# Tail keys' weighted values as 64-row matmuls, and the other weighted-value matmuls fed between feed-forward matmuls

## The chip, the cores and the metric

One core of a Trainium2 chip runs the whole program. Its engines work side by side, each through its own queue in order: PE (matmuls, with weight loads shown apart as PEld), DVE (elementwise), ACT (activation functions, and here copies out of PSUM and the output DMAs), POOL (here it only issues loads) and SP (here it issues transposing DMAs). Matmuls write to PSUM, eight banks of 512 float32 numbers in each of 128 partitions. The metric is the device time of one execution in microseconds (us), the median of three runs.

## The reference

Attention with a bias that depends on the distance of query and key, and behind it a feed-forward layer that multiplies two projections:

```python
scores = q @ k.T / 8 + bias[|i - j|]     # 8 batches, 8 heads, 576 positions, head width 64
attn   = exp(scores) / sum(exp(scores))  # over the keys
x      = attn @ v                        # heads side by side: 4608 tokens of 512
out    = ((x @ w_a) * (x @ w_b)) @ w_out # 512 -> 1536 -> 512
```

The softmax subtracts the row's maximum first, which changes nothing in exact arithmetic; the kernel leaves it out.

## The kernel before

**Tiling of the attention.** The kernel works in pairs of heads: 8 batches of 4 pairs, 32 pairs. A pair's two heads lie on partitions 0 to 63 and 64 to 127 of the transposed queries and keys. The 576 positions are four tiles of 128 and a tail of 64. Scores are computed with keys on the partitions, so that the exponentials are already what the product with v needs as its stationary operand.

For a pair `p` the parts are:

- `qk(p, 0)` and `qk(p, 2)` (L408): scores of key tiles 0, 1 and of 2, 3 against the 512 main queries. Each key tile takes two 64-row matmuls, one for each head, into the two banks of one PSUM tile of the pool `ps_sc` (two such tiles). `ex` (L436) is the exponential on ACT, 1024 columns, into an `at` tile; `mul` (L442) multiplies it on DVE by the bias factor exp(bias).
- the rows: in `qk(p, 2)` also the 64 tail queries against the four main key tiles, eight 64-row matmuls of 64 columns (L424) into two banks, one of each head. `ex_rows` (L428) reads the two banks, `mul_rows` (L533) applies the bias.
- `qk_tail` (L484): the tail keys of both heads (64 partitions each, stacked to 128) against all queries; `ex_tail` (L508) is their exponential, 640 columns, into `att`; `mul_tail` (L526, instruction L531) multiplies its last 256 columns, those of query tile 3 and of the tail queries, by the bias factor. The earlier columns need none.
- the weighted values `av(p, jqs)` (L559): `av_mm` and then `av_norm`. For a query tile `jq`, first the tail keys (L568): 128 rows, the two heads' tail keys one above the other, against a block-diagonal `vt` of 2 x 65 columns. Each 65th column is ones, so that it gives the softmax's denominator. Then for each head and key tile a matmul of 65 columns (L578). For `jq` 4, the tail queries of both heads, four matmuls of 130 columns (L572). Everything accumulates in one PSUM bank with a place for each tile and head, from the pool `ps_av`, which has one bank. `av_norm` (L583) divides on DVE into `XG`: a reciprocal (L589), a product (L591), and for the tail queries two small products (L596). `av(p, (0, 1, 2))` and `av(p, (3, 4))` are two such blocks.
- `t_x` (L600): two transposing DMAs from SP bring `XG` into `xn`, the feed-forward's input.

**Feed-forward.** 4608 tokens are nine chunks of 512. A chunk is 36 units in a fixed list: 24 projections, a first (`ff_a`: four matmuls of 512 columns into a PSUM bank, L642, and a copy on ACT to `ha`, L649) and a second (`ff_b`: four matmuls, and on DVE the product `g` of bank and `ha`, L652) in turn; and 12 output units, four matmuls each (L679), three to a bank, with a copy and an output DMA on ACT after each third. All these banks come from the pool `ps_ff`, which has two.

**Order.** The kernel writes the order of every queue out by hand; nothing is scheduled. Pairs 0 to 7 and the first chunk's projections are an opening of their own. From L868 a loop runs over steps `s` = 8 to 32. Step `s` computes the scores of pair `s` and, for `s` above 8, the weighted values of pair `s - 1`, and places nine feed-forward units between them. `U` is one unit. For `s` not divisible by four the order is:

```python
qk(s,0) ex(s,0) | U1 ex(s,1) av(s-1,(0,1,2)) U2 mul(s,0) U3 mul(s,1)
qk(s,2) + rows, ex(s,2) ex_rows | U4 ex(s,3) U5 mul(s,2) mul_rows
av(s-1,(3,4)) t_x(s-1) U6 U7 mul(s,3) | qk_tail ex_tail U8 U9 mul_tail
```

For `s` divisible by four the second block of weighted values and two more units come before `qk(s,2)`. Loads of later batches and transposing DMAs of queries and keys are issued at a step's end.

With nine units to a step and 36 to a chunk, steps repeat in fours. I call them by `s` modulo four:

| kind | steps | units U1 to U9 |
|---|---|---|
| 1 | 9, 13, ... 29 | first, second, first, ... first |
| 2 | 10, 14, ... 30 | second, first, ... second |
| 3 | 11, 15, ... 31 | first, second, ... second (six), then three output units |
| 0 | 12, 16, ... 28 | nine output units |

Step 32 has no scores: it computes the last pair's weighted values among output units, and transposes on PE (`tr_x`, into `trb`, the one bank of the pool `ps_tr`). The same `trb` takes the first head's rows in each step, a bank of `ps_av` the second's.

Of the kernel before, what the change touches and what calls it, by code (L numbers as in the profile page):

```python
# [13 lines left out]
def kernel(  # L14
# [11 lines left out]
    nc = tc.nc  # L26
    FP32 = mybir.dt.float32
    BF16 = mybir.dt.bfloat16
# [279 lines left out]

    st = [dict() for _ in range(NP)]

    trb = ps_tr.tile([128, 1024], BF16, tag="tr", name="trb")
    turn = [0]

    def tr_half():
        turn[0] ^= 1
        return trb[:, 512 * turn[0]:512 * turn[0] + 512]

    def copy(eng, out, in_):
        if eng is nc.scalar:
# [88 lines left out]
    def qk(p, t0, ts=None):  # L408
        qT, kT, _ = operands(p)
        st[p].setdefault("at", [None] * NM)  # L410
        for t in ts or (t0, t0 + 1):
            ps = ps_sc.tile([128, 2, 512], FP32, tag="sc", name=f"qk{p}_{t}")
            for hh in range(2):
                r = slice(64 * hh, 64 * hh + 64)
                nc.tensor.matmul(out=ps[:, hh, :], lhsT=kT[r, t, :], rhs=qT[r, :, :],  # L415
                                 start=True, stop=True)
            st[p]["ps", t] = ps
        if shared(p) and t0 == 2:
            z = operands(p)[2]
            rows = (trb.bitcast(FP32), ps_av.tile([128, 512], FP32, tag="av", name=f"qr{p}"))  # L420
            for t in range(NM):
                for hh in range(2):
                    r = slice(64 * hh, 64 * hh + 64)
                    nc.tensor.matmul(out=rows[hh][:, ST * t:ST * t + ST], lhsT=kT[r, t, :],  # L424
                                     rhs=z[r, 0, ST * hh:ST * hh + ST], start=True, stop=True)
            st[p]["rows"] = rows

    def ex_rows(p):  # L428
        st[p]["att"] = at = att[p % 2]
        for hh in (1, 0):  # L430
            nc.scalar.activation(
                out=at[:, 0:512].rearrange("p (t h c) -> p h t c", h=2, t=NM)[:, hh, :, :],
                in_=st[p]["rows"][hh][:, 0:256].rearrange("p (t c) -> p t c", t=NM),
                func=ACTF.Exp, scale=scale)

    def ex(p, t):  # L436
        ps = st[p]["ps", t]
        at = atp.tile([128, 2, SM], BF16, tag="at", name=f"at{p}_{t}")
        nc.scalar.activation(out=at[:, :, :], in_=ps[:, :, :], func=ACTF.Exp, scale=scale)  # L439
        st[p]["at"][t] = at  # L440

    def mul(p, t):  # L442
        at, w = st[p]["at"][t], W_sb[p % 4]
        nc.vector.tensor_tensor(out=at[:, :, :], in0=at[:, :, :],  # L444
                                in1=w[:, :, S - 1 + t:S - 1 + t - SM:-1], op=MULT)
# [95 lines left out]
    def weights(p, t, hh, jq):  # L541
        if p >= 4:
            return st[p]["at"][t][:, hh, 128 * jq:128 * jq + 128]
        o = 256 * (t % 2) + 128 * (jq % 2)
        return st[p]["at", jq // 2, t // 2][:, hh, o:o + 128]

    def weights_last(p, t):
        return st[p]["att"][:, 2 * ST * t:2 * ST * t + 2 * ST]

    def weights_tail(p, jq):  # L550
        if jq == 4:
            o = 512 + main_tail(p)
            return st[p]["att"][:, o:o + 2 * ST]
        if p < 4 and jq < 2:
            return atk[:, p, 128 * jq:128 * jq + 128]
        o = 512 + 128 * (jq if p >= 4 else jq - 2)
        return st[p]["att"][:, o:o + 128]
# [2 lines left out]
        av_mm(p, jqs)  # L560
        av_norm(p, jqs)

    def av_mm(p, jqs, pool=None, tag="av"):
        b, hp = divmod(p, 4)
        i = b % 2
        pav = (pool or ps_av).tile([128, 3, 2, Dh + 1], FP32, tag=tag, name=f"av{p}_{jqs[0]}")
        for slot, jq in enumerate(jqs):
            nc.tensor.matmul(out=pav[:, slot, :, :], lhsT=weights_tail(p, jq),  # L568
                             rhs=vt[i][:, :, hp, :], start=True, stop=True)
            if jq == 4:  # L570
                for t in range(NM):
                    nc.tensor.matmul(out=pav[:, slot, :, :], lhsT=weights_last(p, t),  # L572
                                     rhs=vm[i][:, 2 * hp:2 * hp + 2, t, :], start=False,
                                     stop=True, skip_group_check=True)
                continue
            for hh in range(2):
                for t in range(NM):
                    nc.tensor.matmul(out=pav[:, slot, hh, :], lhsT=weights(p, t, hh, jq),  # L578
                                     rhs=vm[i][:, 2 * hp + hh, t, :], start=False,
                                     stop=True, skip_group_check=True)  # L580
        st[p]["pav", jqs[0]] = pav

    def av_norm(p, jqs):  # L583
        pav = st[p]["pav", jqs[0]]
# [15 lines left out]
    def t_x(p, jqs=range(5), eng=None):  # L600
        b, hp = divmod(p, 4)
        c0 = SM * B + ST * b
        if 4 <= p < NP - 1:
            nc.sync.dma_start_transpose(
                out=xn_sb[hp][:, SM * b:SM * b + SM].rearrange("d (j c) -> d j c", j=4),
                in_=XG[p % 2][:, 0:4, :, :].rearrange("p j h d -> p (j h d)"))
            nc.sync.dma_start_transpose(
                out=xn_sb[hp][:, c0:c0 + ST],
                in_=XG[p % 2][0:ST, 4, :, :].rearrange("p h d -> p (h d)"))
            return  # L610
        tr_x(p, jqs)
        copy_x(p, jqs, eng)
# [16 lines left out]


    ff = {"late": False, "n": 0}

    def ff_bank(name):
        ff["n"] += 1
# [4 lines left out]
    def ff_in(w, kind, c, df, lo, n):  # L639
        ps = ff_bank(f"{kind}{c}_{df}_{lo}")  # L640
        for mc in range(NMC):
            nc.tensor.matmul(out=ps[:, 0:n], lhsT=w[df // 4][:, mc, 128 * (df % 4):128 * (df % 4) + 128],  # L642
                             rhs=xn_sb[mc][:, 512 * c + lo:512 * c + lo + n],
                             start=(mc == 0), stop=(mc == NMC - 1))
        ff[kind, df, lo] = ps

    def ff_ha(c, df, lo, n):
# [26 lines left out]
    def ff_o_mm(c, tt, part):  # L674
        if part == 0:
            ff["po", tt] = ff_bank(f"po{c}_{tt}")
        po = ff["po", tt]
        for df in range(4 * part, 4 * part + 4):
            nc.tensor.matmul(out=po[:, :], lhsT=g_sb[df][:, 128 * tt:128 * tt + 128],  # L679
                             rhs=wo_sb[:, df, :], start=(df == 0), stop=(df == NDF - 1))  # L680

    def ff_o_out(c, tt):
        ob = ob_last if (c, tt) == (0, 2) else wrk.tile([128, DM], FP32, tag="ob", name=f"ob{c}_{tt}")
# [43 lines left out]
    def v_next(s):  # L727
        if s % 4 == 0:
            v_in(s // 4, 0, 4)
        if s % 4 == 2:  # L730
            v_in(s // 4, 4, 8)
# [136 lines left out]
    for s in range(8, NP + 1):  # L868
        new = s < NP
        U = "unit"  # L870
        A = lambda *jq: (lambda: av(s - 1, jq) if s > 8 else None)
        steps = []
        if new:
            steps += [lambda: (qk(s, 0), ex(s, 0))]
        if new:
            head = [U, lambda: ex(s, 1), A(0, 1, 2), U, lambda: mul(s, 0), U,
                    lambda: mul(s, 1)]
            late = [A(3, 4), lambda: t_x(s - 1), U]
            if s == 8:
                late = [U]  # L880
            pair = [lambda: v_next(s), lambda: (qk(s, 2), ex(s, 2), ex_rows(s)), U,
                    lambda: ex(s, 3), U, lambda: mul(s, 2), lambda: mul_rows(s)]
            tail = [lambda: (qk_tail(s), ex_tail(s)), U, U, lambda: mul_tail(s)]
            if s % 4 == 0:
                steps += head + late + [U] + pair + [lambda: mul(s, 3)] + tail
            else:
                steps += head + pair + late + [U, lambda: mul(s, 3)] + tail
        else:
            ff["late"] = True
            steps += [A(0, 1, 2), U, U, U, A(3, 4), lambda: t_x(s - 1, (0, 1, 2)), U, U, U,  # L890
                      lambda: t_x(s - 1, (3, 4)), U, U, U]
        b = s // 4 + 1
        if s % 4 == 2 and b < B:
            t_half(b, 0)
        if s % 4 == 0 and 2 <= b - 1 < B:
            t_half(b - 1, 1)
        if s % 4 == 1 and 2 <= b < B:
            load_vt(b)
        for bb in range(3, B):
            for g in range(2):  # L900
                if s == load_slot[bb] + (2 - (bb < 5)) * g:
                    load_half(bb, g)
        quota = 9
        seen, put = 0, 0
        nu = sum(1 for x in steps if x is U)
        for x in steps:
            if x is U:
                seen += 1
                n = (quota * seen + nu - 1) // nu - put
                put_units(n)  # L910
                put += n
            else:
                x()
# [31 lines left out]
```

## Time and profile before

| | |
|---|---|
| time, median of 3 runs | 413.51 us (412.92 to 413.57) |
| profiled execution, first to last instruction (its span) | 412.1 us |
| granted clock of the matrix engine, mean over the span | 1.000 |
| PE busy | 401.5 us, 3420 matmuls |
| DVE busy | 240.6 us |
| ACT busy | 252.0 us |
| feed-forward projections, 880 matmuls (L642) | 23% + 23% of the chain that ended last |
| output matmuls (L679) | 22% of that chain |
| weighted values (L578, L568, L572) | 8% + 2% + 2% of that chain |
| one step of the loop, from start to start | 11.0 us |

Only a part of the profile's time is that of the program's own instructions: the time of a run also holds what lies before the first and after the last. Of the profiled execution no time beside its span is recorded; the median of the runs is 1.4 us above it. A matmul's recorded duration holds its way through the array, and matmuls overlap; what one costs is the distance from its start to the next one's start. A line such as `L578 ... x8` stands for eight instructions that follow each other. In a timeline the brackets give how long an engine was idle before the instruction and what ended that.

### The profile page before, as it was taken

Reading aid. Unit: us, or ns where it says so; the run is one execution under the profiler, and the core shown is the slowest. Engines: PE = TensorE matmul, PEld = TensorE weight load, DVE = VectorE, ACT = ScalarE, POOL = GpSimd, SP = SyncE. Lnnn points to the kernel's source line nnn. Section 1 sums busy time; section 2 is a strip of 40 time slices with the busy share of each in tenths; the row PEclk is TensorE's granted clock in tenths of the full one; section 3 lists DMA queues with packets and bytes.
Section 4 is the critical chain, followed back from the end, with each engine's and each line's share of the span. In section 5 each row is a group of like instructions: output and inputs, shape, how many; then the busy total and the mean of one; then the engine's idle time right before and its main releaser. Section 6 shows DMA issues by size and latency. Waiting matters only on the chain.

```text
span 412.1 us, 8718 instructions
## 1 busy us (share of the span) xinstructions
PE 401.5 (97%) x3420; PEld 209.6 (51%) x3471; DVE 240.6 (58%) x568; ACT 252.0 (61%) x386; POOL 131.4 (32%) x188
## 2 busy tenths in 40 slices
PE   7999999999999999999999999999999999999996
PEld 3476656455554555455445555555445454444443
DVE  4799997366755765476646764567547652421320
ACT  5898992577748665667557765767476642322321
POOL 5966466887029400960069004300000000000000
PEclk9999999999999999999999999999999999999999
DMA  9999999999969924994199908960520012002004
GB/s 152 185 204 197 206 137 148 166 184 131 91 127 157 141 40 91 151 127 94 35 159 150 120 17 136 117 92 17 117 67 17 16 40 78 0 5 98 2 2 102
DMA packets 135962, 42.36 MB, mean 103 GB/s; under 512 B 113544, under 2 KB 131176, under 8 KB 135920
## 3 DMA queue, kind: packets, MB, share of 16 engines
q0 software_dynamic: 81120, 19.88, 54.9%
q1 hardware_dynamic: 49456, 12.61, 19.9%
q10 hardware_dynamic: 5344, 9.31, 7.1%
q8 instruction: 27, 0.44, 0.5%
q14 instruction: 15, 0.12, 0.1%
HBM read 39.23 MB, written 9.45 MB: 118 GB/s over the span
## 4 chain that ended last, share of the span: by engine, by line
PE 95%; DMA 1%; ACT 1%; issue 1%; DVE 0%; ACTq 0%; SPq 0%
PE pb L642 23%; PE pa L642 23%; PE po L679 22%; PE av L578 8%; PE qk L415 7%; PE av L568 2%; PE av L572 2%; PE qkh L455 1%; PE qkt L488 1%; DMA xn<-in_k_dram 1%; PE trb L330 1%; PE trb L424 1%; PE trk L330 1%; ACT ath L461 0%; PE qkt L494 0%
## 5 line engine op out<-in xcount | busy, mean ns | idle before, releaser
L439 ACT ACTIVATE at<-qk 128x1024 bf16<-128x1024 f32 x112 | 113.4, 1029 | 27.4 <-DMA out_dram<-ob 10.3
L652 DVE TENSOR_TENSOR g<-pb,ha 128x512 bf16<-128x512 f32 (+1 forms) x114 | 75.6, 663 | 74.8 <-PE pb L642 58.5
L642 PE MATMUL pb<-xn,wb 128*128 128x512 bf16 (+1 forms) x440 | 111.1, 368 | 0.8
L642 PE MATMUL pa<-xn,wa 128*128 128x512 bf16 (+1 forms) x440 | 110.8, 368 | 0.7
L649 ACT ACTIVATE ha<-pa 128x512 f32<-128x512 f32 (+1 forms) x114 | 66.3, 581 | 67.6 <-PE pa L642 63.8
L679 PE MATMUL po<-wo,g 128*128 128x512 bf16 x403 | 95.5, 379 | 0.8
L444 DVE TENSOR_TENSOR at<-at,W 128x1024 bf16<-128x1024 bf16 x112 | 75.0, 685 | 22.4 <-ACT at L439 22.3
L642 PEld LDWEIGHTS <-wa 128*128 128x128 bf16 x456 | 41.2, 98 | 46.6 <-issue 6.8
L642 PEld LDWEIGHTS <-wb 128*128 128x128 bf16 x456 | 40.6, 98 | 42.9 <-issue 4.7
L679 PEld LDWEIGHTS <-g 128*128 128x128 bf16 x420 | 38.8, 98 | 44.9 <-issue 2.5
L684 ACT ACTIVATE ob<-po 128x512 f32<-128x512 f32 x34 | 20.4, 600 | 40.2 <-PE po L679 30.1
L578 PE MATMUL av<-vm,at 128*128 128x65 bf16 x896 | 41.2, 193 | 0.0
L578 PEld LDWEIGHTS <-at 128*128 128x128 bf16 x896 | 37.4, 97 | 6.1
L174 POOL DMA_DIRECT2D vt<-in_v_dram x12 | 7.4, 622 | 101.9 <-PE av L572 101.1
L136 POOL DMA_DIRECT2D qn<-in_q_dram x48 | 36.6, 825 | 9.2 <-PE trb L501 6.9
L589 DVE RECIPROCAL rc<-av 128x6 f32<-128x6 f32 (+1 forms) x64 | 11.9, 186 | 45.7 <-PE av L578 41.1
L145 POOL DMA_DIRECT2D kn<-in_k_dram x48 | 36.2, 800 | 2.6 <-DMA qn<-in_q_dram 1.6
L568 PE MATMUL av<-vt,att 128*128 128x130 bf16 x152 | 33.6, 221 | 0.2
L415 PE MATMUL qk<-QB,KB 64*128 64x512 bf16 x192 | 29.1, 381 | 0.3
L591 DVE TENSOR_TENSOR XG<-av,rc 128x384 bf16<-128x384 f32 (+2 forms) x64 | 27.2, 425 | 2.2
L515 ACT ACTIVATE att<-qkt 128x640 bf16<-128x640 f32 x24 | 16.8, 701 | 13.0 <-PE qkt L489 13.0
L568 PEld LDWEIGHTS <-att 128*128 128x128 bf16 x152 | 14.9, 98 | 6.4
(105 smaller groups left out, 322.8 us busy)
## 6 DMA issues: line engine op xcount, KB each, us to landing
out_dram<-ob ACTq DMA_DIRECT2D x31, 256.0 KB, 2.9
vn<-in_v_dram POOLq DMA_DIRECT2D x16, 256.0 KB, 5.7
kn<-in_k_dram POOLq DMA_DIRECT2D x48, 64.0 KB, 4.9
qn<-in_q_dram POOLq DMA_DIRECT2D x48, 64.0 KB, 4.1
wa<-in_moe_w_a_dram POOLq DMA_DIRECT2D x3, 512.0 KB, 8.9
wb<-in_moe_w_b_dram POOLq DMA_DIRECT2D x3, 512.0 KB, 8.3
wo<-in_moe_w_out_dram POOLq DMA_DIRECT2D x1, 1536.0 KB, 15.7
xn<-XG SPq DMA_TRANSPOSE x52, 3.5
```

Of the source, the lines that this page charges most:

```text
L136: nc.gpsimd.dma_start(out=by_tile(qn[b % 2])[:, h0 // 4, t, :, :], in_=q[b, h0:h1, 128 * t:128 * t + 128, :].transpose([1, 0, 2]))
L145: nc.gpsimd.dma_start(out=by_tile(kn[b % 2])[:, h0 // 4, t, :, :], in_=k[b, h0:h1, t:SM:NM, :].transpose([1, 0, 2]))
L415: nc.tensor.matmul(out=ps[:, hh, :], lhsT=kT[r, t, :], rhs=qT[r, :, :], start=True, stop=True)
L439: nc.scalar.activation(out=at[:, :, :], in_=ps[:, :, :], func=ACTF.Exp, scale=scale)
L444: nc.vector.tensor_tensor(out=at[:, :, :], in0=at[:, :, :], in1=w[:, :, S - 1 + t:S - 1 + t - SM:-1], op=MULT)
L568: nc.tensor.matmul(out=pav[:, slot, :, :], lhsT=weights_tail(p, jq), rhs=vt[i][:, :, hp, :], start=True, stop=True)
L578: nc.tensor.matmul(out=pav[:, slot, hh, :], lhsT=weights(p, t, hh, jq), rhs=vm[i][:, 2 * hp + hh, t, :], start=False, stop=True, skip_grou ...
L591: nc.vector.tensor_tensor(out=xg[:, jqs[0]:jqs[0] + m, :, :], in0=pav[:, 0:m, :, 0:Dh], in1=rc[:, 0:m, :].unsqueeze(3).to_broadcast([128, ...
L642: nc.tensor.matmul(out=ps[:, 0:n], lhsT=w[df // 4][:, mc, 128 * (df % 4):128 * (df % 4) + 128], rhs=xn_sb[mc][:, 512 * c + lo:512 * c + lo ...
L649: nc.scalar.activation(out=ha[:, 0:n], in_=ff["pa", df, lo][:, 0:n], func=ACTF.Copy)
L652: nc.vector.tensor_tensor(out=g_sb[df][:, lo:lo + n], in0=ff["pb", df, lo][:, 0:n], in1=ff["ha", df, lo][:, 0:n], op=MULT)
L679: nc.tensor.matmul(out=po[:, :], lhsT=g_sb[df][:, 128 * tt:128 * tt + 128], rhs=wo_sb[:, df, :], start=(df == 0), stop=(df == NDF - 1))
```

## The change

1. The rows' two banks come from a helper `two_banks` (one of `ps_tr`, one of `ps_av`), which the weighted values use as well. `trb` becomes a list with one tile, so that step 32 can take a new one.
2. From step 9 to 31 the weighted values of pair `s - 1` have a bank for each head. `av_tails` computes the tail keys: for each of the five query tiles two matmuls of 64 rows and 65 columns, one for each head on its half of the partitions, into the two banks. It stands right behind `qk(s, 0)`.
3. `av_head` lists a head's other matmuls, 20 of 65 columns: five query tiles by four key tiles. For the tail queries this is one matmul for each head and key tile, where one of 130 columns served both heads.
4. `feed_av` puts both heads' lists, each head's division (`norm_head`) and `t_x` into a queue of 43 entries. `feed_some`, called after every feed-forward matmul, takes 44/12 entries per matmul from it, so that they are spread over the twelve matmuls of U1 to U3. `feed_all` empties what is left.
5. Step order: the former blocks of weighted values are gone, and the order is the same for all `s`: four units before `qk(s, 2)`, five after it.

```diff
+    def av_tails(p):
+        b, hp = divmod(p, 4)
+        st[p]["av2"] = banks = two_banks(f"av{p}")
+        for jq in range(5):
+            for hh in range(2):
+                r = slice(64 * hh, 64 * hh + 64)
+                nc.tensor.matmul(out=banks[hh][:, J * jq:J * jq + J], lhsT=weights_tail(p, jq)[r, :],
+                                 rhs=vt[b % 2][r, hh, hp, :], start=(jq == 0), stop=True,
+                                 skip_group_check=True)
+
+    def av_head(p, hh):
+        b, hp = divmod(p, 4)
+        bank, v = st[p]["av2"][hh], vm[b % 2]
+
+        def mm(jq, t):
+            w = weights_last(p, t) if jq == 4 else weights(p, t, hh, jq)
+            return lambda: nc.tensor.matmul(out=bank[:, J * jq:J * jq + J], lhsT=w,
+                                            rhs=v[:, 2 * hp + hh, t, :], start=False, stop=True,
+                                            skip_group_check=True)
+
+        return [mm(jq, t) for jq in range(5) for t in range(NM)]
+
+    def norm_head(p, hh):
+        x = st[p]["av2"][hh][:, 0:5 * J].rearrange("p (j d) -> p j d", d=J)
+        rc = wrk.tile([128, 5], FP32, tag="rc2", name=f"rh{p}_{hh}")
+        nc.vector.reciprocal(out=rc[:, :], in_=x[:, :, Dh])
+        nc.vector.tensor_tensor(out=XG[p % 2][:, 0:4, hh, :], in0=x[:, 0:4, 0:Dh],
+                                in1=rc[:, 0:4].unsqueeze(2).to_broadcast([128, 4, Dh]), op=MULT)
+        rows = slice(ST * hh, ST * hh + ST)
+        nc.vector.tensor_tensor(out=XG[p % 2][0:ST, 4, hh, :], in0=x[rows, 4, 0:Dh],
+                                in1=rc[rows, 4:5].to_broadcast([ST, Dh]), op=MULT)
...
+    def feed_some():
+        feed["due"] += feed["rate"]
+        while feed["q"] and feed["due"] >= 1:
+            feed["due"] -= 1
+            feed["q"].pop(0)()
+        if not feed["q"]:
+            feed["due"] = 0.0
...
+    def feed_av(p, matmuls):
+        feed["q"] = [*av_head(p, 0), lambda: norm_head(p, 0), *av_head(p, 1), lambda: norm_head(p, 1),
+                     lambda: t_x(p)]
+        feed["rate"], feed["due"] = (len(feed["q"]) + 1) / matmuls, 0.0
...
-            steps += [lambda: (qk(s, 0), ex(s, 0))]
+            steps += [lambda: (qk(s, 0), av_tails(s - 1) if s > 8 else None, ex(s, 0))]
         if new:
-            head = [U, lambda: ex(s, 1), A(0, 1, 2), U, lambda: mul(s, 0), U,
+            head = [lambda: feed_av(s - 1, 12) if s > 8 else None, U, lambda: ex(s, 1), U, lambda: mul(s, 0), U,
                     lambda: mul(s, 1)]
-            late = [A(3, 4), lambda: t_x(s - 1), U]
-            if s == 8:
-                late = [U]
-            pair = [lambda: v_next(s), lambda: (qk(s, 2), ex(s, 2), ex_rows(s)), U,
+            late = [U]
+            pair = [feed_all, lambda: v_next(s), lambda: (qk(s, 2), ex(s, 2), ex_rows(s)), U,
                     lambda: ex(s, 3), U, lambda: mul(s, 2), lambda: mul_rows(s)]
-            tail = [lambda: (qk_tail(s), ex_tail(s)), U, U, lambda: mul_tail(s)]
-            if s % 4 == 0:
-                steps += head + late + [U] + pair + [lambda: mul(s, 3)] + tail
-            else:
-                steps += head + pair + late + [U, lambda: mul(s, 3)] + tail
+            tail = [lambda: (qk_tail(s), ex_tail(s)), U, U, feed_all, lambda: mul_tail(s)]
+            steps += head + late + pair + [U, lambda: mul(s, 3)] + tail
```

`feed_some()` is added at the end of the matmul loops of `ff_in` (L641) and `ff_o_mm` (L678).

More of the change, by code (lines that the diff above doesn't have):

```diff
@@ L309 @@
     st = [dict() for _ in range(NP)]
-    trb = ps_tr.tile([128, 1024], BF16, tag="tr", name="trb")
+    trb = [ps_tr.tile([128, 1024], BF16, tag="tr", name="trb")]
     turn = [0]
@@ L315, in tr_half, with two_banks @@
         turn[0] ^= 1
-        return trb[:, 512 * turn[0]:512 * turn[0] + 512]
+        return trb[0][:, 512 * turn[0]:512 * turn[0] + 512]
+    def two_banks(name):
+        return (ps_tr.tile([128, 512], FP32, tag="tr", name=f"{name}_0"),
+                ps_av.tile([128, 512], FP32, tag="av", name=f"{name}_1"))
     def copy(eng, out, in_):
@@ L419, in qk @@
             z = operands(p)[2]
-            rows = (trb.bitcast(FP32), ps_av.tile([128, 512], FP32, tag="av", name=f"qr{p}"))
+            rows = two_banks(f"qr{p}")
             for t in range(NM):
@@ L561, in av, with av_list, mm, put @@
         av_norm(p, jqs)
-    def av_mm(p, jqs, pool=None, tag="av"):
+    def av_list(p, jqs, pool=None, tag="av"):
         b, hp = divmod(p, 4)
         i = b % 2
-        pav = (pool or ps_av).tile([128, 3, 2, Dh + 1], FP32, tag=tag, name=f"av{p}_{jqs[0]}")
+        def mm(slot, hh, start, lhsT, rhs):
+            def put():
+                if ("pav", jqs[0]) not in st[p]:
+                    st[p]["pav", jqs[0]] = (pool or ps_av).tile([128, 3, 2, Dh + 1], FP32, tag=tag,
+                                                                name=f"av{p}_{jqs[0]}")
+                out = st[p]["pav", jqs[0]][:, slot, :, :] if hh is None else st[p]["pav", jqs[0]][:, slot, hh, :]
+                nc.tensor.matmul(out=out, lhsT=lhsT, rhs=rhs, start=start, stop=True,
+                                 skip_group_check=not start)
+            return put
+        todo = []
         for slot, jq in enumerate(jqs):
-            nc.tensor.matmul(out=pav[:, slot, :, :], lhsT=weights_tail(p, jq),
-                             rhs=vt[i][:, :, hp, :], start=True, stop=True)
+            todo.append(mm(slot, None, True, weights_tail(p, jq), vt[i][:, :, hp, :]))
             if jq == 4:
                 for t in range(NM):
-                    nc.tensor.matmul(out=pav[:, slot, :, :], lhsT=weights_last(p, t),
-                                     rhs=vm[i][:, 2 * hp:2 * hp + 2, t, :], start=False,
-                                     stop=True, skip_group_check=True)
+                    todo.append(mm(slot, None, False, weights_last(p, t), vm[i][:, 2 * hp:2 * hp + 2, t, :]))
                 continue
@@ L577, in av_mm @@
                 for t in range(NM):
[L578 to L581, printed above, removed]
+                    todo.append(mm(slot, hh, False, weights(p, t, hh, jq), vm[i][:, 2 * hp + hh, t, :]))
+        return todo
+    def av_mm(p, jqs, *pool):
+        for put in av_list(p, jqs, *pool):
+            put()
+    J = Dh + 1
+    def av_tails(p):
[25 more added lines that the diff above has]
+                                in1=rc[rows, 4:5].to_broadcast([ST, Dh]), op=MULT)
     def av_norm(p, jqs):
@@ L631, with feed_all @@
     ff = {"late": False, "n": 0}
+    feed = {"q": [], "rate": 0.0, "due": 0.0}
+    def feed_some():
[5 more added lines that the diff above has]
+            feed["due"] = 0.0
+    def feed_all():
+        while feed["q"]:
+            feed["q"].pop(0)()
+    def feed_av(p, matmuls):
+        feed["q"] = [*av_head(p, 0), lambda: norm_head(p, 0), *av_head(p, 1), lambda: norm_head(p, 1),
+                     lambda: t_x(p)]
+        feed["rate"], feed["due"] = (len(feed["q"]) + 1) / matmuls, 0.0
     def ff_bank(name):
@@ L644, in ff_in @@
                              start=(mc == 0), stop=(mc == NMC - 1))
+            feed_some()
         ff[kind, df, lo] = ps
@@ L680, in ff_o_mm @@
                              rhs=wo_sb[:, df, :], start=(df == 0), stop=(df == NDF - 1))
+            feed_some()
     def ff_o_out(c, tt):
@@ L873 @@
         if new:
-            steps += [lambda: (qk(s, 0), ex(s, 0))]
+            steps += [lambda: (qk(s, 0), av_tails(s - 1) if s > 8 else None, ex(s, 0))]
         if new:
-            head = [U, lambda: ex(s, 1), A(0, 1, 2), U, lambda: mul(s, 0), U,
+            head = [lambda: feed_av(s - 1, 12) if s > 8 else None, U, lambda: ex(s, 1), U, lambda: mul(s, 0), U,
                     lambda: mul(s, 1)]
-            late = [A(3, 4), lambda: t_x(s - 1), U]
-            if s == 8:
-                late = [U]
-            pair = [lambda: v_next(s), lambda: (qk(s, 2), ex(s, 2), ex_rows(s)), U,
+            late = [U]
+            pair = [feed_all, lambda: v_next(s), lambda: (qk(s, 2), ex(s, 2), ex_rows(s)), U,
                     lambda: ex(s, 3), U, lambda: mul(s, 2), lambda: mul_rows(s)]
-            tail = [lambda: (qk_tail(s), ex_tail(s)), U, U, lambda: mul_tail(s)]
-            if s % 4 == 0:
-                steps += head + late + [U] + pair + [lambda: mul(s, 3)] + tail
-            else:
-                steps += head + pair + late + [U, lambda: mul(s, 3)] + tail
+            tail = [lambda: (qk_tail(s), ex_tail(s)), U, U, feed_all, lambda: mul_tail(s)]
+            steps += head + late + pair + [U, lambda: mul(s, 3)] + tail
         else:
             ff["late"] = True
+            trb[0] = ps_tr.tile([128, 1024], BF16, tag="tr", name="trz")
             steps += [A(0, 1, 2), U, U, U, A(3, 4), lambda: t_x(s - 1, (0, 1, 2)), U, U, U,
```

## The prediction

> **What bounds the kernel now.** I read the page first: the engines' shares, then the chain of work that ended last.
>
> ```profile
> span 412.1 us, 8718 instructions
> PE 401.5 (97%) x3420; PEld 209.6 (51%) x3471; DVE 240.6 (58%) x568; ACT 252.0 (61%) x386; POOL 131.4 (32%) x188
> PE 95%; DMA 1%; ACT 1%; issue 1%; DVE 0%; ACTq 0%; SPq 0%
> ```
>
> The matrix engine (PE) is 95% of the chain; DVE and ACT hold under 2% of it. So a nanosecond put on PE's queue is a nanosecond of the span, and so is any wait of PE. Then the timeline of PE, in the loop over pairs, for a step of kind 1 (start us, duration, engine, line):
>
> ```profile
> 259.25 0.61 PE L415 MATMUL qk<-QB,KB 64*128 64x512 bf16 x4
> 259.79 1.04 PE L642 MATMUL pa<-xn,wa 128*128 128x512 bf16 x4
> 260.66 0.22 PE L568 MATMUL av<-vt,att 128*128 128x130 bf16 x1
> 260.72 0.42 PE L578 MATMUL av<-vm,at 128*128 128x65 bf16 x8
> 260.98 0.22 PE L568 MATMUL av<-vt,att 128*128 128x130 bf16 x1
> ...
> 263.43 0.61 PE L415 MATMUL qk<-QB,KB 64*128 64x512 bf16 x4
> 263.87 0.19 PE L424 MATMUL trb<-ZB,KB 64*128 64x64 bf16 x1
> 263.88 0.19 PE L424 MATMUL qr<-ZB,KB 64*128 64x64 bf16 x1
> 263.90 0.19 PE L424 MATMUL trb<-ZB,KB 64*128 64x64 bf16 x1
> ...
> 266.20 0.40 PE L572 MATMUL av<-vm,att 128*128 128x130 bf16 x4
> 266.43 1.02 PE L642 MATMUL pb<-xn,wb 128*128 128x512 bf16 x4
> ...
> 268.16 0.38 PE L488 MATMUL qkt<-QB,ZB 128*128 128x512 bf16 x1
> ```
>
> Durations overlap; what a matmul costs is the distance of starts. A feed-forward matmul of 512 columns costs 0.216 us (four from 266.43 end at 267.29). A tail matmul (L568) costs 0.060 (260.66 to 260.72), eight weighted-value matmuls (L578) 0.26, so 0.032 each, four of the last queries (L572) 0.23, so 0.058 each. 64-row matmuls on two row halves run in pairs: the rows (L424) come 0.01 and 0.02 apart, 0.03 a pair. A change between 64 and 128 rows costs about 0.10: two score pairs are 0.43, but 0.54 lies between 259.25 and 259.79. Step starts (first L415) lie at 259.25, 270.25, 281.26, 292.26, 303.27: 11.0 us each, all kinds alike, PE never waiting.
>
> **The change part by part.** The new form of the weighted values is in 23 steps (9 to 31).
>
> Matmuls. Removed per step: 5 tails at 0.060 and 4 last-query matmuls at 0.058, 0.53 us. Added: 5 pairs of 64-row tails at 0.030, and 8 last-query matmuls of 65 columns at 0.032, 0.41. The tails follow the first scores, which are 64-row already, so no row change is added. Saved 0.126 a step, 23 times: -2.9 us.
>
> Interleaving. Forty matmuls of 65 columns now stand between the twelve feed-forward matmuls of three units, in groups of three or four. A group's borders are in the trace: an av start is 0.216 after the feed-forward start before it (34 of 34 in the steps), and a feed-forward start follows the last av of a block by 0.033 (L578 to L642). So I price it at nothing. Bounds: an av matmul cannot cost less than its columns' share of a feed-forward one, 65/512 of 0.216 = 0.027, against 0.032: 40 x 23 x 0.0047 = 4.3 us of gain; at the other end every one of the 12 x 23 = 276 returns to feed-forward exposes a load, as the row change does (0.10): 28 us of loss. The nearest row is the 0.033, the same two shapes in the same order, so nothing it is. The Trainium skill (TensorE: Matmul & The Clock Gate, Part 3, The mechanism) says that a weight load overlaps a running matmul only when the row groups differ. All these matmuls use the same rows, so by that rule each border would show a load of 0.097 us, some 24 a step, +54 us. The trace shows the reverse: loads are hidden at equal rows, and seen at the row change.
>
> First new wait: tails on the product of the tail keys (DVE, L531). The tails moved from behind a unit to right behind the first scores, so they need L531 of the step before much earlier. DVE and PE at the start of a step of kind 3:
>
> ```profile
> 280.30 1.03 PE L642 MATMUL pb<-xn,wb 128*128 128x512 bf16 x4
> 281.26 0.60 PE L415 MATMUL qk<-QB,KB 64*128 64x512 bf16 x4
> 281.44 0.69 DVE L652 TENSOR_TENSOR g<-pb,ha 128x512 bf16<-128x512 f32 x1 [0.60 <-PE pb L642]
> 282.04 0.28 DVE L531 TENSOR_TENSOR att<-att,Wt 128x256 bf16<-128x256 bf16 x1
> ```
>
> The last unit of kind 2 is a second projection; its product g stands ahead of L531 on DVE and cannot begin before that unit's last matmul. L531 ends at 282.32, 1.06 after the step's start. It writes the keys' last 256 columns, which are query tiles 3 and 4 of the tails; three pairs may run before. PE reaches the fourth at 0.43 + 3 x 0.03 = 0.52. With about 0.06 for the signal (DVE to the first waiting PE work in the opening) and 0.09 for a load that now stands open, it starts at 1.21: 0.69 lost, and everything of PE's queue behind it, the feed-forward with it. The chain hangs on PE's own last matmul, so it moves with PE and cannot be outrun. Kind 3 comes at steps 11, 15, ... 31, 6 times: +4.1. In the other kinds L531 ends at 0.38 (kind 1), 0.20 (kind 2) and -0.60 (kind 0): no wait.
>
> Second new wait: feed-forward banks behind ACT's exponentials. Before, four units and a block of av matmuls (0.6 us) stood between the second scores and the tail scores, which lie 263.43 to 268.16 = 4.73 us apart. Now the block and one unit lie ahead of the second scores; what remains is scores, rows and row change (0.64) and three units (2.59): 3.23. ACT's work in the stretch is unchanged:
>
> ```profile
> 274.44 0.60 PE L415 MATMUL qk<-QB,KB 64*128 64x512 bf16 x4
> 274.87 1.02 ACT L439 ACTIVATE at<-qk 128x1024 bf16<-128x1024 f32 x1 [0.59 <-PE qk L415]
> 275.79 0.38 ACT L431 ACTIVATE att<-qr 128x256 bf16<-128x256 f32 x1
> 276.05 0.39 ACT L431 ACTIVATE att<-trb 128x256 bf16<-128x256 f32 x1
> 276.32 0.62 ACT L649 ACTIVATE ha<-pa 128x512 f32<-128x512 f32 x1
> ```
>
> In kinds 1 and 3 unit 5 is a first projection; its copy to ha stands behind these, and unit 7 takes its PSUM bank. From the second scores' start: 0.43 to the exponential, 0.92 + 0.26 + 0.27 for it and the rows' two, 0.60 for the copy, 0.06 signal: 2.54. PE is there at 0.64 + 2 x 0.864 = 2.37. Lost 0.17, twelve times: +2.0. In kind 2 the built program has unit 5 wait for unit 4's copy, with only 0.95 us of PE work from that unit's last matmul start, against 0.42 + 0.60 + 0.06 = 1.08: 0.13; and unit 7 wait for unit 5's product, 1.08 of PE work against 0.49 + 0.69 + 0.06 = 1.24: 0.16. Together 0.29, six times: +1.7. Kind 0 is output units alone: none. Bounds of all these: nothing, if ACT and DVE are a fifth of a us earlier than I reckon, to twice as much (+7.4); I take the sums, each being rows end to end.
>
> At no cost: the division, two reciprocals, two products of 256 columns and two of 64x64, is as long on DVE as before (about 1.5 us) and DVE idles over 40%; if that cover goes, the rows of the next scores wait, having some 0.4 us of slack. The transposing DMAs of XG leave no later than before, the loads of vt are released earlier; POOL's and SP's queues hold nothing else new. Steps divisible by four and step 8 move one unit, all feed-forward of the same length.
>
> Sum: -2.9 + 4.1 + 2.0 + 1.7 = +4.9 us, against the profiled execution's span of 412.1; this execution lies 1.4 below the runs' median of 413.5, which I take as work around the span that stays. 413.5 + 4.9 = 418.4.
>
> **Rivals.** Only the first wait binds, ACT and DVE keep up: 413.5 - 2.9 + 4.1 = 414.7. For it: ACT is 61% busy, margins of 0.13 to 0.17 are thin. Against: the order of ACT's queue is fixed.
>
> Not slower: the av matmuls run at their columns' rate between feed-forward matmuls, whose 0.216 hides their loads: 418.4 - 4.3 = 414.1, no change that can be told, and with waits a little smaller, below. For it: loads last 0.097 and blocks of av may be paced by them. Against: every av but one in three or four still follows another. It decides from 0.027 per matmul, 5 ns under the row.
>
> Loads exposed at the returns: each 0.010 us costs 276 x 0.010 = 2.8; at 0.015, 422.5. Against: the 0.033 row.
>
> The change does not pair the tails: ten at 0.030 instead of five pairs, 0.15 x 23 = +3.4: 421.8. Against: rows in the same two banks pair at L424.
>
> **How the numbers follow.** Forecast (416 to 421) 0.55; first wait alone 0.17; not slower 0.16; exposed loads or unpaired tails 0.12. The range leaves a tenth on each side: 413.3, where the not-slower case has its better half below, to 422. Within the forecast alone: 416.0 to 421. About 0.2% (0.8 us) is what a measurement can tell: faster 0.10 and same 0.07, both out of the not-slower case (and the low edge of the first-wait one), slower 0.83.
>
> **What the profile after would show.** Right: PE waits on L531's product once in each kind-3 step, 0.6 to 0.7 us, six times; PE waits on ACT's copy before unit 7 in kinds 1 and 3; steps of 11.05, 11.17, 11.74 and 10.88 us for kinds 1, 2, 3, 0; tails 0.03 a pair; PE's other idle unchanged. Wrong: av starts under 0.030 apart or returns over 0.04 change the price of interleaving; step lengths equal at 10.9 mean that no wait binds. A wait of the rows on the second head's division would be one that I have priced at nothing.

## The result, and the profile after

The changed kernel takes 418.06 us (median of four, 417.54 to 418.97) against 413.54 for the kernel before beside it: a ratio of 1.011 (95% interval 1.0093 to 1.0127). The forecast was 418.4. The profiled execution of the changed kernel has a granted clock of 0.990 over its span against 1.000 before; the difference lies in the opening, after which step 9 starts 0.84 us earlier (82.32 against 83.16), and from step 9 on both have 1.00. One single execution of all those reported below, of the kernel with the product of the tail keys earlier, took 2271 us, and its ratio leaves that one out.

From the page of the changed kernel, the same three lines as of the kernel before:

```profile
span 415.8 us, 9144 instructions
PE 400.7 (96%) x3618; PEld 208.6 (50%) x3678; DVE 241.7 (58%) x568; ACT 252.9 (61%) x386; POOL 131.4 (32%) x188
PE 91%; DVE 3%; issue 1%; DMA 1%; ACT 1%; ACTq 1%; SPq 0%; DVEq 0%
```

PE's share of the chain fell from 95% to 91%, and DVE, which had none, has 3%: the chain now leaves PE for work of DVE. PE's busy time tells nothing: it fell by 0.8 us while the time rose, and both profiles miss records of matmuls (3420 where there are 3471 weight loads before, 3618 where there are 3678 after).

Where PE waits in the loop, the list of waits names (engine and line, what released it; us in total, times, longest):

```profile
PE av L605 <- DVE att L535: 2.6, 6, 0.4
PEld L605 <- DVE att L535: 3.3, 6, 0.5
```

L605 are the tails, L535 is `mul_tail`'s product (L531 before): six times, as many as there are steps of kind 3. The page counts a wait from the modelled end of the last matmul; by starts it is longer, as the timeline of one such step shows (PE, PEld and DVE; step 27):

```profile
281.91 1.03 PE L708 MATMUL pb<-xn,wb 128*128 128x512 bf16 x4
282.87 0.60 PE L419 MATMUL qk<-QB,KB 64*128 64x512 bf16 x4
283.04 0.69 DVE L719 TENSOR_TENSOR g<-pb,ha 128x512 bf16<-128x512 f32 x1 [0.71 <-PE pb L708]
283.31 0.26 PE L605 MATMUL av<-vt,att 64*128 64x65 bf16 x6
283.65 0.28 DVE L535 TENSOR_TENSOR att<-att,Wt 128x256 bf16<-128x256 bf16 x1
283.98 0.12 PEld L605 LDWEIGHTS <-att 64*128 64x128 bf16 x4 [0.55 <-DVE att L535]
283.99 0.24 PE L605 MATMUL av<-vt,att 64*128 64x65 bf16 x4 [0.42 <-DVE att L535]
284.16 0.39 PE L708 MATMUL pa<-xn,wa 128*128 128x512 bf16 x1
```

Six tails run at once; the last four wait for L535, which ends at 283.93, 1.06 after the step's start, as before the change. The seventh tail starts 1.12 after the step's start, 0.585 later than the 0.03 a pair would have it.

The starts of five steps, kinds 1, 2, 3, 0, 1 (the timeline of PE, first scores):

```profile
260.77 0.61 PE L419 MATMUL qk<-QB,KB 64*128 64x512 bf16 x4
271.78 0.60 PE L419 MATMUL qk<-QB,KB 64*128 64x512 bf16 x4
282.87 0.60 PE L419 MATMUL qk<-QB,KB 64*128 64x512 bf16 x4
294.47 0.60 PE L419 MATMUL qk<-QB,KB 64*128 64x512 bf16 x4
305.33 0.61 PE L419 MATMUL qk<-QB,KB 64*128 64x512 bf16 x4
```

That is 11.01, 11.09, 11.60 and 10.86 us, where all kinds took 11.00 or 11.01. Kind 0, in which PE waits for nothing, shows what the matmuls save: 0.145. The other kinds give it back in waits: 0.145 in kind 1, 0.23 in kind 2 and 0.74 in kind 3.

Kind 1 has one short wait, and kind 3 has it beside that of the tails. The timeline of a step of kind 1 (step 25; units 5, 6, 7 on PE, with DVE and ACT):

```profile
266.47 0.70 DVE L448 TENSOR_TENSOR at<-at,W 128x1024 bf16<-128x1024 bf16 x1
266.93 1.04 PE L708 MATMUL pa<-xn,wa 128*128 128x512 bf16 x4
267.19 0.69 DVE L719 TENSOR_TENSOR g<-pb,ha 128x512 bf16<-128x512 f32 x1
267.94 1.02 PE L708 MATMUL pb<-xn,wb 128*128 128x512 bf16 x3
268.16 0.62 ACT L716 ACTIVATE ha<-pa 128x512 f32<-128x512 f32 x1
268.83 0.59 PE L708 MATMUL pa<-xn,wa 128*128 128x512 bf16 x2
```

Unit 6 (pb) starts 1.01 after unit 5, where it is 0.88 when nothing waits (the kernel with DVE's order alone, below); it starts 0.06 after the end of unit 4's product g (267.19 + 0.69 = 267.88), which stood on DVE behind the second head's division and `mul(s,1)` (L448). Unit 7 starts 0.05 after the end of unit 5's copy (268.78).

Kind 2 has two short waits. The timeline of a step of it (step 26; units 5 and 7 on PE, with ACT's copy of unit 4 and DVE's products of units 3 and 5):

```profile
277.39 0.60 ACT L716 ACTIVATE ha<-pa 128x512 f32<-128x512 f32 x1 [1.63 <-PE pa L708]
277.47 0.69 DVE L719 TENSOR_TENSOR g<-pb,ha 128x512 bf16<-128x512 f32 x1
278.04 1.02 PE L708 MATMUL pb<-xn,wb 128*128 128x512 bf16 x4
279.17 0.69 DVE L719 TENSOR_TENSOR g<-pb,ha 128x512 bf16<-128x512 f32 x1
279.91 1.02 PE L708 MATMUL pb<-xn,wb 128*128 128x512 bf16 x4
```

Unit 5 starts 0.05 after the end of unit 4's copy (277.99) and before the end of unit 3's product (278.16), so it waited for the copy, about 0.10. Unit 7 starts 0.05 after the end of unit 5's product (279.86), about 0.15 late.

### The profile page after: what moved, and what is told of

It reads as the page before. It is cut to its first block, busy times and chain, and to the rows that moved or that the text cites. A ratio compares the mean times of both kernels' runs of the same rounds, so it can differ in the third digit from the quotient of the medians.

```text
span 415.8 us, 9144 instructions
## 1 busy us (share of the span) xinstructions
PE 400.7 (96%) x3618; PEld 208.6 (50%) x3678; DVE 241.7 (58%) x568; ACT 252.9 (61%) x386; POOL 131.4 (32%) x188
## 4 chain that ended last, share of the span: by engine, by line
PE 91%; DVE 3%; issue 1%; DMA 1%; ACT 1%; ACTq 1%; SPq 0%; DVEq 0%
PE pb L708 23%; PE pa L708 23%; PE po L746 22%; PE av L615 8%; PE qk L419 7%; PE av L577 3%; PE qkt L492 1%; DVE g L719 1%; DMA xn<-in_k_dram 1%; PE av L605 1%; PE qkh L459 1%; DVE ath L474 1%; PE qr L428 1%; PE trb L334 1%; PE trk L334 1%
## 5 line engine op out<-in xcount | busy, mean ns | idle before, releaser
L708 PE MATMUL pa<-xn,wa 128*128 128x512 bf16 (+1 forms) x439 | 119.5, 368 | 0.5
L708 PE MATMUL pb<-xn,wb 128*128 128x512 bf16 (+1 forms) x429 | 116.0, 367 | 1.1
L746 PE MATMUL po<-wo,g 128*128 128x512 bf16 x406 | 101.2, 379 | 0.5
L448 DVE TENSOR_TENSOR at<-at,W 128x1024 bf16<-128x1024 bf16 x112 | 76.4, 685 | 8.0 <-ACT at L443 7.3
L708 PEld LDWEIGHTS <-wb 128*128 128x128 bf16 x456 | 42.5, 97 | 38.9 <-issue 7.1
L615 PE MATMUL av<-vm,at 128*128 128x65 bf16 x736 | 60.5, 194 | 0.1
L615 PEld LDWEIGHTS <-at 128*128 128x128 bf16 x736 | 45.6, 97 | 24.6
L624 DVE RECIPROCAL rh<-av 128x5 f32<-128x5 f32 x46 | 9.0, 195 | 55.6 <-PE av L615 55.6
L615 PE MATMUL av<-vm,att 128*128 128x65 bf16 x184 | 20.7, 194 | 1.2
L625 DVE TENSOR_TENSOR XG<-av,rh 128x256 bf16<-128x256 f32 x46 | 19.5, 425 | 1.6
L465 ACT ACTIVATE ath<-qkh 128x1024 bf16<-128x1024 f32 x16 | 15.8, 1024 | 2.1 <-PE qkh L459 1.8
```

Of the source, the lines that this page charges most:

```text
L448: nc.vector.tensor_tensor(out=at[:, :, :], in0=at[:, :, :], in1=w[:, :, S - 1 + t:S - 1 + t - SM:-1], op=MULT)
L615: return lambda: nc.tensor.matmul(out=bank[:, J * jq:J * jq + J], lhsT=w, rhs=v[:, 2 * hp + hh, t, :], start=False, stop=True, skip_group_ ...
L625: nc.vector.tensor_tensor(out=XG[p % 2][:, 0:4, hh, :], in0=x[:, 0:4, 0:Dh], in1=rc[:, 0:4].unsqueeze(2).to_broadcast([128, 4, Dh]), op=MULT)
```

## The experiments

The theory: PE's stream of matmuls got shorter, and the loss is three orders of queues: the product of the tail keys comes too late on DVE, and around the second scores DVE's products and ACT's copies give the feed-forward's banks back too late. Its rivals: the loss is in the matmuls themselves (their number, their interleaving), or the waits are only handed on when one is taken away. All kernels below are the changed kernel with one edit, and each ratio is to the kernel before run beside it.

**The product of the tail keys one unit earlier.**

```diff
-            tail = [lambda: (qk_tail(s), ex_tail(s)), U, U, feed_all, lambda: mul_tail(s)]
+            tail = [lambda: (qk_tail(s), ex_tail(s)), U, lambda: mul_tail(s), U, feed_all]
```

> The product of the tail keys is written one unit earlier in DVE's order, ahead of the last unit's product g; nothing else changes. If the wait of the tails on it costs what the profile after shows (0.585 us in each of six kind-3 steps, 3.5 us), the wait goes and the time falls from 418.1 to about 414.6; steps of kind 3 fall from 11.60 to about 11.02 us, the others stay. If the loss lies in the matmuls themselves (one more weight load or column than reckoned), nothing moves: 418.1. If the wait is only handed on, because DVE now stands still for the tail keys' exponential and the last g comes late, about half: 416 to 417, and the next step's second unit waits for its bank.

Measured: 414.94, ratio 1.0024 (1.0013 to 1.0035), 3.1 us less than the changed kernel; by the ratios it is 3.6, since the kernel before took 414.04 beside this run and 413.54 beside the changed one. Its steps of kind 3 take 11.01 us. PE, PEld and DVE at the start of one (step 27):

```profile
279.51 1.03 PE L708 MATMUL pb<-xn,wb 128*128 128x512 bf16 x4
279.86 0.29 DVE L535 TENSOR_TENSOR att<-att,Wt 128x256 bf16<-128x256 bf16 x1
280.47 0.60 PE L419 MATMUL qk<-QB,KB 64*128 64x512 bf16 x4
280.65 0.69 DVE L719 TENSOR_TENSOR g<-pb,ha 128x512 bf16<-128x512 f32 x1 [0.50 <-PE pb L708]
280.91 0.31 PE L605 MATMUL av<-vt,att 64*128 64x65 bf16 x10
281.16 0.39 PE L708 MATMUL pa<-xn,wa 128*128 128x512 bf16 x1
```

The product now runs while PE is in the last unit, all ten tails go through in one stretch, and the last g starts as soon after its matmuls as before. The wait is gone and not handed on.

**DVE's and ACT's orders around the second scores.**

```diff
-            head = [..., U, lambda: mul(s, 0), U,
-                    lambda: mul(s, 1)]
-            late = [U]
-            pair = [feed_all, lambda: v_next(s), lambda: (qk(s, 2), ex(s, 2), ex_rows(s)), U,
-                    lambda: ex(s, 3), U, lambda: mul(s, 2), lambda: mul_rows(s)]
+            head = [..., U, lambda: mul(s, 0), U]
+            late = [U, lambda: mul(s, 1)]
+            pair = [feed_all, lambda: v_next(s), lambda: (qk(s, 2), ex(s, 2)), U,
+                    lambda: ex_rows(s), lambda: ex(s, 3), U, lambda: mul(s, 2), lambda: mul_rows(s)]
```

> Only orders on DVE and ACT: the second product of the scores (mul(s,1)) stands behind unit 4 instead of ahead of it, and the rows' two exponentials behind unit 5's copy instead of ahead of it. If the short waits before units 6 and 7 come from these two queues, kinds 1 and 3 lose their 0.13 to 0.16 us and kind 2 a part of its 0.25: twelve times 0.15, 1.8 us and up to 1 us more, 418.1 to about 416. If they come from the bank that the pool gives out, nothing moves.

Measured: 415.85, ratio 1.0044 (1.0033 to 1.0055), 2.2 us less (2.7 by the ratios). Steps of kind 1 fall to 10.85 and of kind 3 to 11.45, 0.15 each, in eleven of the twelve (step 21 stays at 11.01 in this profile); kind 2 stays at 11.09.

**Each of the two orders alone.** Two kernels: only `mul(s, 1)` moved behind unit 4 (DVE), and only `ex_rows` moved behind unit 5 (ACT).

> Only DVE's order: mul(s,1) behind unit 4. In the profile after, unit 6 of kinds 1 and 3 waits 0.13 us for unit 4's product, and unit 7 then 0.03 for ACT's copy of unit 5. If the copy is a wait of its own that lies in the shadow of the product's, the steps of kinds 1 and 3 stay at 11.01 and 11.60, PE now waiting some 0.16 before unit 7: 418.1. If DVE's queue is the whole cause: 10.86 and 11.45, twelve times 0.15 less, 416.3.

> Only ACT's order: the rows' exponentials behind unit 5's copy. If both waits are there and overlap, 0.03 us goes in each step of kinds 1 and 3 and the 0.13 before unit 6 stays: steps of 10.98 and 11.57, 417.7. If ACT's queue is the whole cause, 10.86 and 11.45, 416.3. The wait of kind 3's tails stays in both cases.

Measured: DVE alone 418.61, ratio 1.0115 (1.0101 to 1.0130); ACT alone 418.06, ratio 1.0103 (1.0088 to 1.0118). Neither differs from the changed kernel by more than the intervals; the traces do tell them apart. With DVE's order alone (units 5, 6, 7 of step 25, and ACT's copy):

```profile
267.45 1.04 PE L708 MATMUL pa<-xn,wa 128*128 128x512 bf16 x4
268.33 1.03 PE L708 MATMUL pb<-xn,wb 128*128 128x512 bf16 x4
268.68 0.62 ACT L716 ACTIVATE ha<-pa 128x512 f32<-128x512 f32 x1
269.35 0.81 PE L708 MATMUL pa<-xn,wa 128*128 128x512 bf16 x3
```

Unit 6 comes 0.88 after unit 5, its wait gone, and unit 7 now comes 1.02 after unit 6, held by the copy that ends at 269.30. The step takes 11.01 as before. With ACT's order alone:

```profile
266.52 1.04 PE L708 MATMUL pa<-xn,wa 128*128 128x512 bf16 x4
267.53 1.02 PE L708 MATMUL pb<-xn,wb 128*128 128x512 bf16 x4
267.60 0.60 ACT L716 ACTIVATE ha<-pa 128x512 f32<-128x512 f32 x1 [0.27 <-PE pa L708]
268.39 1.03 PE L708 MATMUL pa<-xn,wa 128*128 128x512 bf16 x4
```

Unit 6 still waits, 1.01 after unit 5; unit 7 waits for nothing (0.86). The steps fall by 0.03, to 10.98 and 11.58. So there are two waits of nearly the same length, 0.13 on DVE and 0.155 on ACT. Each hides the other: taking away one gains nothing or 0.03, taking away both gains 0.15.

**Both kinds of order together.** The edits of the first two experiments.

> Both orders together. If the two kinds of wait are apart from each other the gains add up: 418.1 - 3.5 - 2 to -3 = 411.6 to 412.6, below the kernel before (413.5), with steps of 10.86 us in kinds 0, 1 and 3 and about 11.05 in kind 2. If one wait hides behind the other, 413.5 or more.

Measured: 412.33, ratio 0.9960 (0.9948 to 0.9972). Steps of kinds 0, 1 and 3 take 10.85 or 10.86. The gains are separate and add up: 3.1 + 2.2 = 5.3 by the two alone and 5.7 together, and in the profiles, from step 9's start to step 32's, 3.4 + 1.7 against 5.4, where single longer steps of the two alone are the difference. With both the change is faster than the kernel before, by 0.4%.

**Both, and the weighted values spread over ten matmuls.**

```diff
-            head = [lambda: feed_av(s - 1, 12) if s > 8 else None, U, ...
+            head = [lambda: feed_av(s - 1, 10) if s > 8 else None, U, ...
```

> The two orders of before (product of the tail keys first; DVE's and ACT's queues), and the av matmuls spread over ten feed-forward matmuls instead of twelve, so that the second division and the products behind it start 0.4 us earlier. If the 0.10 us before unit 5 in kind 2 hangs on that queue, kind 2 falls from 11.09 to 10.99: 412.3 - 0.6 = 411.7. The wait before unit 7 of kind 2 hangs on two second projections one unit apart and stays at 0.15. If neither moves, 412.3.

Measured: 412.11, ratio 0.9954 (0.9941 to 0.9966). The time does not differ from the last one's by more than the interval, but the steps of kind 2 do (starts of kinds 1, 2, 3, 0, 1):

```profile
257.32 0.61 PE L419 MATMUL qk<-QB,KB 64*128 64x512 bf16 x4
268.18 0.61 PE L419 MATMUL qk<-QB,KB 64*128 64x512 bf16 x4
279.19 0.60 PE L419 MATMUL qk<-QB,KB 64*128 64x512 bf16 x4
290.05 0.61 PE L419 MATMUL qk<-QB,KB 64*128 64x512 bf16 x4
300.92 0.61 PE L419 MATMUL qk<-QB,KB 64*128 64x512 bf16 x4
```

Kind 2 takes 11.01 instead of 11.09, the others 10.86: the 0.10 before unit 5 went, the 0.15 before unit 7 is the one wait left. By the trace of step 26 unit 5 now waits for unit 3's product instead of unit 4's copy, and that product has ended 0.21 us before unit 5 starts (274.14 and 274.35): the built program gives unit 5 the other bank.

**The weighted values as two blocks.** The same order, but `feed_some` gives head 0's 20 matmuls and division in one go behind the sixth feed-forward matmul, head 1's behind the twelfth.

```diff
-        feed["due"] += feed["rate"]
-        while feed["q"] and feed["due"] >= 1:
-            feed["due"] -= 1
-            feed["q"].pop(0)()
-        if not feed["q"]:
-            feed["due"] = 0.0
+        feed["due"] += 1
+        for _ in range({6: 21, 12: 22}.get(feed["due"], 0)):
+            if feed["q"]:
+                feed["q"].pop(0)()
...
-        feed["rate"], feed["due"] = (len(feed["q"]) + 1) / matmuls, 0.0
+        feed["due"] = 0
```

> The changed kernel with each head's 20 matmuls as one block: head 0 behind the sixth feed-forward matmul of units 1 to 3, head 1 behind the twelfth, with the division, the DMAs and all orders on the other engines as they were. If interleaving is worth nothing on PE, as I priced it, 418.1 plus at most the 0.02 us a step that the spacings of the traces make (0.0321 in a block before, 0.031 to 0.033 between feed-forward matmuls now): 418.1 to 418.6. If the feed-forward matmuls hide the av matmuls' loads, so that interleaving gains its bound of 0.0047 each: 422. If every return to feed-forward costs something, blocks are faster: 0.01 us each is 2.8 us, 415.3.

Measured: 418.36, ratio 1.0111 (1.0097 to 1.0126), no difference from the changed kernel that the times can tell. The trace tells one: every kind of step is 0.02 longer than in the changed kernel (11.03, 11.11, 11.63, 10.88). In blocks an av matmul starts 0.032 after the last one on average, between feed-forward matmuls 0.031. So interleaving is worth 0.02 us a step, 0.5 in all: neither the gain of 4.3 nor a loss.

**Tails on all 128 rows.**

```diff
-                nc.tensor.matmul(out=banks[hh][:, J * jq:J * jq + J], lhsT=weights_tail(p, jq)[r, :],
-                                 rhs=vt[b % 2][r, hh, hp, :], start=(jq == 0), stop=True,
+                nc.tensor.matmul(out=banks[hh][:, J * jq:J * jq + J], lhsT=weights_tail(p, jq),
+                                 rhs=vt[b % 2][:, hh, hp, :], start=(jq == 0), stop=True,
```

> The ten tail matmuls read all 128 rows (the other head's rows are zeros in vt), so that they can't run in pairs; the rest is the changed kernel. If the pairs cost 0.03 us and a 128-row matmul of 65 columns 0.032, a step gets 0.17 us longer, less where the wait of kind 3 hides it: 17 x 0.17 + 6 x 0.07 = 3.3, 421.4. If 64-row matmuls save nothing here, the same 418.1.

Measured: 420.68, ratio 1.0151 (1.0136 to 1.0166). The ten tails behind the first scores of a step of kind 1 (step 29), in the changed kernel and on all rows:

```profile
305.33 0.61 PE L419 MATMUL qk<-QB,KB 64*128 64x512 bf16 x4
305.77 0.31 PE L605 MATMUL av<-vt,att 64*128 64x65 bf16 x10
```

```profile
307.10 0.61 PE L419 MATMUL qk<-QB,KB 64*128 64x512 bf16 x4
307.64 0.48 PE L605 MATMUL av<-vt,att 128*128 128x65 bf16 x10
307.95 0.38 PE L708 MATMUL pa<-xn,wa 128*128 128x512 bf16 x1
```

The ten take 0.17 longer. The change between 64 and 128 rows, 0.10, now stands ahead of the tails (0.54 behind the scores' start, against 0.44) and no longer behind them. Steps of kinds 0, 1 and 2 are 0.15 longer (11.01, 11.16 and 11.25). In kind 3 (11.56) the wait for L535 takes up the loss: it falls from 0.585 to 0.39. Pairing by row halves is real and is worth 0.15 us a step where nothing hides it.

## Why the prediction was right

The time and its direction were right, and so was the mechanism: the matmuls save time on PE, and a tail product that comes late on DVE, with two short waits for feed-forward banks, costs more than that. That the time came within 0.3 is in part luck, as the last point shows. Term by term, for the loop:

| term | forecast, us | measured, us |
|---|---|---|
| matmuls, a step | -0.126 | -0.145 |
| tails wait for L531, a step of kind 3 | 0.69 | 0.585 |
| kinds 1 and 3, units 6 and 7, a step | 0.17 | 0.15 |
| kind 2, units 5 and 7, a step | 0.29 | 0.24 |
| the loop's sum | +4.9 | +3.6 |

- Matmuls: the blocks' kind-0 step, 0.125 under the step before, is the forecast's term to a thousandth or two; the other 0.02 is the interleaving, which I had priced at nothing. By the Trainium skill's sentence that a weight load overlaps a running matmul only when the row groups differ (TensorE: Matmul & The Clock Gate, Part 3, The mechanism), each of the 24 borders a step would have cost another 0.097, as the prediction worked out. The borders took 0.216 into an av matmul and 0.033 out of one, as before the change, so for these shapes the word "only" does not hold. I had left out that the same section also lets a load run ahead when it goes to a background weight buffer, which would allow this.
- First wait: the place, the cause and the six times are right, the size is 0.1 too long. The step that failed is the load "that now stands open", 0.09: the seventh tail's load and its matmul start within 0.01 of each other in the timeline, 0.06 after L535's end. The signal is the whole delay.
- Second waits: the sum is right and the reason, in kinds 1 and 3, was half of it. I had unit 7 wait for ACT's copy; in the profile it is unit 6 that waits, for DVE's product. I had put the division at no cost, since DVE idles over 40%, and had not added up its queue behind the second division: a step that failed, and luck that the size fits. The copy's wait was there as well, 0.155 by the kernel with DVE's order alone against my 0.17, but hidden except for 0.03. In kind 2 both waits are where I had them, 0.10 and 0.15 against 0.13 and 0.16.
- Rivals: the first wait alone (414.7) is nearest to the kernel with DVE's and ACT's orders, 415.85, which still has kind 2's waits, and is not the change. Av matmuls at their columns' rate and exposed loads are refuted by the blocks (interleaving is worth 0.02 a step, where by the one it would gain 0.19 and by the other lose), unpaired tails by the tails on all rows.
- The sum over the loop was 1.3 too high, and the time nevertheless only 0.3. From step 9's start to step 32's the changed kernel lost 3.6 us in its profile: -0.145 x 23 + 0.585 x 6 + 0.15 x 12 + 0.24 x 6 = 3.4, and 0.2 in step 14, which takes 11.32. There unit 9 starts 0.23 late, for the product of unit 7, which begins on DVE 0.40 us after its wait for PE had ended (0.04 in step 18). What held it the trace does not show; every kernel with twelve matmuls has it, and the one with ten does not (11.01). The medians lie 4.5 apart, so 0.9 is outside the loop. In the profiles it is at the very end, which I had at nothing: from step 32's start to the last instruction they have 75.92 before and 76.83 after. So an overestimate of the loop and an oversight at the end nearly cancel. (The two spans lie only 3.7 apart, since the opening of the one profile is 0.84 shorter, as said above.) The issues of the last output DMAs on ACT, before and after (min/median/max in ns):

```profile
L691 ACTq DMA_DIRECT2D out_dram<-ob x6: 473/572/615, 401.0 to 406.7; - x6
```

```profile
L759 ACTq DMA_DIRECT2D out_dram<-ob x6: 473/578/1532, 403.8 to 409.4; - x6
```

One issue of 1.53 us holds up ACT's last copy by 0.92. Of the nine profiles of the changed form eight have such an issue at this place, 1.30 to 1.85 us; in the ninth, the kernel with the product first, it takes 0.61 as before, and the next one 0.86 instead of 0.50. The one profile of the kernel before has neither. So it may go with the changed program, though not with the way in which the weighted values are fed, since the blocks have it too (1.74). Its cause stays open, and chance is not excluded.

## What to carry to other kernels

When one engine's stream is full, a shorter stream can be worth nothing until the queues that feed it are read again. List, for each instruction that moves forward, what it reads last, and add up the queue of the engine that writes it. Here one line moved by one unit was worth as much as the whole saving (3.4 and 3.3 us by the steps). Two waits of like length that follow each other hid one another here, so try their cures together before one is called useless.

## What I had not expected

- Av matmuls of 65 columns between feed-forward matmuls start 0.029 to 0.036 apart, 0.031 on average, against 0.032 in a block.
- One DMA issue on ACT took 1.53 us where 0.57 is usual, and eight of nine profiles of the changed form have the like.
- DVE's wait and ACT's wait, on different engines and before different units, fell within 0.03 us of each other in length.
